# A gate in front of the third group's loads, a last copy and store in two halves, and a new order, in an RWKV attention and SmeLU feed-forward kernel

## The chip, the core and the metric

The kernel runs on one core of a Trainium2 chip. The metric is the device time of one execution in microseconds (us). The core has five engines that run their own instruction queues in order and wait for each other by semaphores: TensorE (PE, with its weight loads, PEld), VectorE (DVE), ScalarE (ACT), GpSimd (POOL) and SyncE (SP), which here only issues DMAs.

## What is computed

The reference takes r, k, v of shape (4, 8, 768, 48), a decay w and a bonus u per head and channel, and two weight matrices. It runs a linear attention with a decaying state over 768 positions, puts the heads of a position side by side (384 channels), and sends the 3072 rows through a feed-forward layer:

```python
for t in range(S):
    cur = einsum('bhd,bhe->bhde', u * k[t], v[t])
    y[t] = einsum('bhd,bhde->bhe', r[t], state + cur)
    state = w * state + einsum('bhd,bhe->bhde', k[t], v[t])
h = x @ w_in                      # x: (3072, 384), w_in: (384, 2048)
g = where(h >= 1, h, where(h <= -1, 0, (h + 1) ** 2 / 4))
out = g @ w_out                   # w_out: (2048, 384)
```

## The kernel before

The positions are cut into 6 chunks of 128 and the 4 batch rows into 2 pairs, which gives 12 groups. A group has two units (one batch row of one chunk: 128 positions, 8 heads). For a group the kernel makes scaled copies of r and k (Rs, Ks: r times a rising, k times a falling power of w), the bonus term (KU = k u, RKU = r KU, `us` sums it over channels, B multiplies it into v, giving V2), turns Rs and Ks so that channels lie on partitions (T, TR, TK on TensorE, or RT, KT by a DMA transpose from group 4 on), and multiplies them to A, the 128 x 128 matrix of each head. AT is A under a triangular mask in bf16. Y is AT times v, plus Rs times the state; `y` adds V2. Sp is the chunk's own contribution to the state, which Tm and decay fold in. Each y is turned to xT (X and xc, or by a DMA transpose, xcg).

The feed-forward layer goes in four pieces q of 512 hidden columns: m (12 matmuls of 256 columns, L464) into a pair of PSUM banks, then r and s (the clamped square on ScalarE, r sometimes on VectorE), then g on VectorE (L487), then M (per unit 4 matmuls of 384 columns, L499) into the output banks. A word such as M0.12 in the order is group 0, unit 1, piece 2. After the last M of a group, o or og copies the result out of PSUM and st or stg stores it through SP. For the last group (11) the two units are copied and stored apart.

w_in comes in three pieces (1, 1 and 2 of the four q, L243), w_out in two (2 and 2, L246), both through GpSimd's queue, which turns float32 into bf16 on the way. All loads of r, k and v (L252) go through SP in the order of the words LR, LK, LV. Groups 0 to 2 are loaded in half pieces (one unit), most of the others whole. Word Z issues filler matmuls on a tile of zeros (L526).

There is no scheduler. ORDER is a list of words, each one step, and the engines' queues follow the order of the words. A word may name the PSUM banks after a slash and the engine after "=" (V, A or G for VectorE, ScalarE, GpSimd). Buffers come from pools with a fixed number of slots (SLOTS), and a step that takes a slot again waits for the readers of what was in it. In this order the loads of group 2 (LR2.0, LR2.1) stand right behind the three words for w_in, followed on SP by LK2.0, LK2.1, LK3 and LR3.

Of the kernel before, what the change touches and what calls it, by code (L numbers as in the profile page):

```python
# [24 lines left out]
Zs/0 ln Z19 bw/1 LK0.0 bu/0 uS=V LK1.0 LR0.0 LK0.1 LR0.1 LV0.0 wq/2 WdnS Ks1.0=G LR1.0 LR1.1 Wdn/3 Ks0.0=V Ks0.1=V  # L25
TK0/0 Wup/1 Rs0.0=V TR0/3 LK1.1 cK0=A WupS KU0.1=G KU0.0=V RKU0.0=G cR0=A KU1.0=G LV0.1 Rs0.1=V Z2 TR1/1 A0/03 LV1.0
LV1.1 WI0 WI1 WI2 us0.0 cR1=A TK1/1 cK1=A AT0.1 Z4 A1/13 Rs1.0=V LR2.0 LR2.1 Rs1.1=V V0.1 AT1.0 V0.0 Z9 TR3/1 B0.0=G
AT1.1 RKU0.1=V wE AT0.0 wC=A us0.1 Z7 Y1/3 TR2/0 B0.1=G Y0/2 y0 y1 cR2=A RKU1.0=G Z8 X0/2 Z4 TK2/3 X1/0 Ks1.1=G xc0=A
Sp1/2 cK2=A xc1=A Z7 TK3/3 cK3=A Tm1 A2/20 m0.0/0 cR3=V us1.0 AT2.1 AT2.0 r0.0=A A3/31 AT3.1 KU1.1=G RKU1.1=G m0.1/1
V1.0 s0.0=A B1.0=G Sp2/2 AT3.0 us1.1 r0.1=A Tm2 Y2/3 y2 g0.0 V1.1 X2/0 LK2.0 Y3/1 B1.1=G s0.1=A LK2.1 Sp0/2 Sp3/3  # L30
xc2=V LK3 y3 WO0 m0.3/0 r0.3=A s0.3=A g0.1 X3/1 Tm0 xc3=V m0.2/1 LR3 LV2.0 Tm3 m1.1/2 g0.3 r1.1=V m1.0/3 m1.2/0 Ks2=G
r0.2=A s0.2=A g0.2 sbf2=A s1.1=A r1.0=A s1.0=A sbf3=A g1.1 m1.3/1 r1.2=V WO1 KU2=G LV2.1 M0.00/2 M0.10 M0.11 M0.01
g1.0 M1.00/3 M1.10 M1.11 M1.01 Rs2=G s1.2=A g1.2 T5/0 RKU2=G LK4 r1.3=A s1.3=A g1.3 T4/1 LV3 Ks3=G M0.02 M0.03 LR4 us2
c5=V A5/0 KU3=G Rs3=G c4=V A4/1 AT5 sbf1=A M1.02 M0.12 M0.13 AT4 T6/0 sbf0=A V2 Y4/1 Y5 B2=G og0=A T7/2 c6=A RKU3=G
c7=A yg2 LV5 M1.12 Sp4/0 Sp5 M1.03 X5/2 Tmg2 decayg2=G X4/1 M1.13 A6/0 xc4=A xc5=V m2.0/2 A7/1 us3 AT6 m2.1/0 og1=A
LK5 LR5 V3 Y6/3 B3=G sbfg2=A r2.0=A AT7 Y7 m2.2/1 s2.0=A Ks4=G yg3 xcg3 m2.3/3 g2.0 Rs4=G r2.1=A s2.1=A g2.1 LV4
r2.2=A s2.2=A KT4 M2.00/2 M2.10 M2.01 M2.11 r2.3=A KU4=G RT4 RKU4=G g2.2 s2.3=A LK6 m3.0/0 us4 M2.02 m3.1/1 LR6 M2.12
LV6 r3.0 s3.0=A Ks5=G g2.3 M2.03 Sp6/3 Sp7 M2.13 g3.0 m3.2/0 Rs5=G Tmg3 r3.1 s3.1=A RT5 og2=A g3.1 V4 AA4/23 AT9 Ks6=G
r3.2 s3.2=A KT5 m3.3/1 M3.00/3 M3.10 V5 B4=G AT8 Y8/2 Y9 r3.3 g3.2 s3.3=A LK8 M3.11 M3.12 M3.01 M3.02 yg4 AA5/20 g3.3
M3.13 M3.03 xcg4 m4.0/1 LR7 KU5=G RKU5=G AT10 LK7 decayg3=G sbfg3=A Rs6=G og3=A us5 LV7 B5=G KU6=G RKU6=G r4.0 Sp8/2  # L40
Sp9 AT11 Tmg4 m4.1/3 s4.0=A Y10/0 Y11 yg5 m4.2/2 r4.1 g4.0 xcg5 RT6 s4.1=A g4.1 m4.3/0 r4.2 us6 KT6 r4.3 LV8 s4.2=A
g4.2 M4.00/1 M4.10 M4.01 stg0 M4.11 s4.3=A g4.3 m5.1/3 Ks7=G V7 M4.12 LR8 decayg4=G Rs7=G AA6/02 M4.02 M4.03 M4.13
r5.1 AT12 m5.0/0 s5.1=A V6 sbfg4=A stg2 AT13 Y12/2 Y13 stg1 og4=V m5.2/1 g5.1 KU8=G B6=G yg6 m5.3/3 KT7 xcg6 Sp10/2
r5.0 s5.0=A KU7=G RKU7=G r5.2 s5.2=A Sp11 g5.0 M5.00/0 M5.10 M5.11 M5.01 RT7 Tmg5 LR9 g5.2 M5.02 Ks8=G LK9 us7 r5.3
s5.3=A V8 g5.3 decayg5=G sbfg5=A LK11 m6.1/2 r6.1 s6.1=A stg3 Rs8=G RT8 B7=G AA7/13 M5.03 Rs9=G M5.12 M5.13 AT15
m6.0/3 og5=A r6.0 AT14 g6.1 Y14/0 Y15 yg7 RKU8=G KU9=G xcg7 s6.0=A m6.3/1 m6.2/2 g6.0 Sp12/0 Sp13 r6.3 r6.2 s6.2=A us8
# [8 lines left out]
us11 AA11/12 B11=G r10.0 s10.0=A AT23 M9.12 M9.03 M9.13 AT22 m10.1/2 g10.0 sbfg9=A Y22/1 Y23 og9=A r10.1 stg9 s10.1=A
yg11 xcg11 m10.3/0 M10.00/3 g10.1 M10.10 r10.3 m10.2/1 s10.3=A g10.3 r10.2 M10.11 M10.01 s10.2=A m11.0/2 g10.2 r11.0
m11.1/0 M10.02 M10.03 r11.1 s11.0=A m11.2/1 g11.0 M10.12 M10.13 s11.1=A r11.2 g11.1 m11.3/2 og10=V s11.2=A M11.10/0
M11.11 g11.2 stg10 r11.3 s11.3=A M11.00/3 M11.01 M11.12 M11.02 g11.3 M11.13 M11.03 o11.1=V st11.1 o11.0=A st11.0
# [15 lines left out]
def kernel(  # L74
# [35 lines left out]
    def copy(e, out, in_):  # L110
        nc.scalar.copy(out, in_) if e == "A" else engines[e].tensor_copy(out, in_)  # L111
# [20 lines left out]
    idle = const.tile([P, 512], BF16, name="idle")  # L132
# [116 lines left out]
    def load(x, what, cls, g, j):  # L249
        j0, j1 = by_unit(g, j)  # L250
        t = make(cls, (what, g), [P, UNITS * H, D], F32)
        nc.sync.dma_start(out=t[:, j0 * H : j1 * H, :], in_=source(x, g, j0, j1))  # L252

# [237 lines left out]
    def do_M(e, b, g, jq):  # L491
        j, q = jq
        last = g == S // C * BP - 1
        key, k = (("op", g, j), 0) if last else (("op", g), j)
        if key not in tiles:
            tiles[key] = pair(b[0], F32, "op")
        wi, wo = part(q, OUT_PARTS)
        for f in range(FG):
            nc.tensor.matmul(  # L499
                tiles[key][:, k, :DO], tiles["g", g, q][:, f, j * P : (j + 1) * P], w_out_sb[wi][:, wo, f * DO : (f + 1) * DO],  # L500
                start=(q == 0 and f == 0), stop=(q == nQ - 1 and f == FG - 1),
            )
# [21 lines left out]
    def do_Z(e, b, n):  # L524
        for i in range(n):
            nc.tensor.matmul(tiles["z"][:, 0, :P], idle[:, :P], idle[:, :P], start=True, stop=True)  # L526

# [39 lines left out]
```

## Time and profile before

| | |
|---|---|
| median of 3 runs | 174.8 us (174.24 to 174.95) |
| the profiled execution's own time | 173.8 us |
| its span, first to last instruction | 172.0 us |
| TensorE busy | 163.7 us (95%) |
| VectorE, ScalarE, GpSimd busy | 130.6, 130.0, 117.1 us |
| DMA | 28.26 MB, 103591 packets, mean 164 GB/s |
| last matmul's end to the span's end | 3.5 us |

Times in the profile count from the start of the span. A row of the timeline gives start, length, engine, line, operation, output and inputs, shapes, and in brackets the idle time of the engine ahead of it with what ended that wait. "x3" says that a row stands for three neighbours. A row of DMA issues says when the issuing engine handed the transfer over; "DMA to landing" is the time from there until its data had arrived (least, median, most). The program's filler matmuls count as busy TensorE time.

### The profile page before, as it was taken

The page shows a single profiled execution, that of the slowest core. Times are in us where ns is not written, and L with a number is a line of the kernel's source. Part 1 is how long each engine was busy: PE and PEld are TensorE (multiplying, and loading weights), DVE is VectorE, ACT ScalarE, POOL GpSimd, SP SyncE. Part 2 cuts the span into 40 slices and gives each one's busy share as a digit, 9 for nine tenths or more (in the row PEclk, how much of TensorE's full clock was granted, in tenths as well). Part 3 has the DMA queues.
Part 4 walks back from the last instruction along what each step waited for, and adds up shares of the span by engine and source line. Part 5 has one row for each costly group of instructions (what it writes and reads, how often), then busy time and mean ns, then how long its engine had stood idle before and what let it go on. Part 6 is the DMA issues. An engine that isn't in the chain of part 4 may idle for free.

```text
span 172.0 us, 4014 instructions
## 1 busy us (share of the span) xinstructions
PE 163.7 (95%) x1658; PEld 130.9 (76%) x1658; DVE 130.6 (76%) x149; ACT 130.0 (76%) x150; POOL 117.1 (68%) x85
## 2 busy tenths in 40 slices
PE   7989968999999999989999999999999999999991
PEld 5768768956889778588787797696897787888850
DVE  4578798988687688859799779885889958873751
ACT  4356588991699899289979878689695896988941
POOL 3496755998589959999999998999577804300000
PEclk9999999999999999999999999999999999999999
DMA  5999999999995999999999998998999034130022
GB/s 106 198 187 191 199 203 197 221 195 203 174 190 88 213 188 175 188 204 150 200 312 197 185 215 174 219 173 168 308 195 219 4 60 138 43 98 0 8 91 91
DMA packets 103591, 28.26 MB, mean 164 GB/s; under 512 B 98834, under 2 KB 102676, under 8 KB 103572
## 3 DMA queue, kind: packets, MB, share of 16 engines
q1 hardware_dynamic: 101824, 24.85, 79.6%
q0 software_dynamic: 1744, 3.15, 10.0%
q8 instruction: 13, 0.21, 0.5%
q14 instruction: 6, 0.05, 0.1%
q10 hardware_dynamic: 4, 0.00, 0.0%
HBM read 20.45 MB, written 4.72 MB: 146 GB/s over the span
## 4 chain that ended last, share of the span: by engine, by line
PE 81%; DMA 5%; SPq 4%; ACT 3%; POOL 2%; DVE 2%; issue 1%; DVEq 0%; POOLq 0%
PE hp L464 36%; PE op L499 34%; SPq L252 4%; PE A L359 3%; DMA Vi<-in_v_dram 3%; DMA xT<-y 2%; PE Y L427 2%; PE Y L421 2%; PE Sp L394 2%; ACT pt L475 1%; ACT Vb L111 1%; POOL V L302 1%; PE T L319 1%; DVE g L487 1%; POOL RKU L271 1%
## 5 line engine op out<-in xcount | busy, mean ns | idle before, releaser
L464 PE MATMUL hp<-xT,w_in 128*128 128x256 bf16 x576 | 69.1, 273 | 0.9 <-DMA xT<-y 0.5
L499 PE MATMUL op<-w_out,g 128*128 128x384 bf16 x384 | 68.4, 326 | 0.0
L487 DVE SCALAR_TENSOR_TENSOR g<-sq,hp 128x1024 bf16<-128x1024 bf16 x48 | 57.9, 1215 | 13.2 <-ACT sq L484 13.2
L464 PEld LDWEIGHTS <-w_in 128*128 128x128 bf16 x576 | 61.9, 114 | 4.2 <-issue 1.2
L475 ACT ACTIVATE pt<-hp 128x1024 f32<-128x1024 f32 x46 | 46.9, 1020 | 14.0 <-PE hp L464 14.0
L499 PEld LDWEIGHTS <-g 128*128 128x128 bf16 x384 | 36.3, 98 | 21.3
L484 ACT ACTIVATE sq<-pt 128x1024 bf16<-128x1024 f32 x46 | 48.3, 1057 | 1.2
L368 DVE TENSOR_TENSOR AT<-A,umask 128x1024 bf16<-128x1024 f32 x20 | 23.7, 1219 | 5.2 <-PE A L359 5.2
L271 POOL TENSOR_TENSOR Ks<-Ki,Wdn 128x768 bf16<-128x768 f32 (+1 forms) x12 | 20.2, 1684 | 7.4 <-DMA Ki<-in_k_dram 3.7
L302 POOL TENSOR_TENSOR V<-Vb,diag 128x768 f32<-128x768 bf16 (+1 forms) x14 | 18.1, 1292 | 10.2 <-DVE diag L293 4.4
L271 POOL TENSOR_TENSOR RKU<-Ri,KU 128x768 f32<-128x768 f32 (+1 forms) x13 | 21.2, 1631 | 1.2 <-DVE KU L271 0.8
L405 POOL TENSOR_TENSOR state<-Tm,wCm 128x768 f32<-128x768 f32 x8 | 14.6, 1822 | 10.6 <-DVE Tm L402 10.6
L271 POOL TENSOR_TENSOR KU<-Ki,u_sb 128x768 f32<-128x768 f32 (+1 forms) x13 | 21.2, 1632 | 0.4 <-DMA Ki<-in_k_dram 0.3
L271 POOL TENSOR_TENSOR Rs<-Ri,Wup 128x768 bf16<-128x768 f32 x10 | 18.2, 1824 | 0.0
L439 DVE TENSOR_TENSOR y<-Y,V 128x768 bf16<-128x768 f32 x10 | 9.6, 956 | 5.9 <-PE Y L427 3.3
L111 ACT CAST Vb<-Vi 128x768 bf16<-128x768 f32 (+1 forms) x14 | 10.2, 734 | 4.8 <-DMA Vi<-in_v_dram 4.8
L293 DVE TENSOR_REDUCE diag<-RKU 128x16 f32<-128x768 f32 (+1 forms) x14 | 11.6, 830 | 1.5 <-POOL RKU L271 1.5
L111 ACT COPY o<-op 128x768 f32<-128x768 f32 (+1 forms) x9 | 6.9, 764 | 6.4 <-PE op L499 6.3
L111 ACT CAST state_bf<-state 128x768 bf16<-128x768 f32 (+1 forms) x12 | 8.5, 717 | 3.7 <-POOL state L405 3.7
L427 PE MATMUL Y<-Vb,AT 128*128 128x48 bf16 x192 | 10.2, 185 | 0.4 <-ACT Vb L111 0.4
L427 PEld LDWEIGHTS <-AT 128*128 128x128 bf16 x192 | 9.3, 97 | 0.7 <-issue 0.5
L402 DVE TENSOR_TENSOR Tm<-Sp,state 128x768 f32<-128x768 f32 x8 | 7.6, 956 | 2.7 <-PE Sp L394 2.7
(73 smaller groups left out, 121.2 us busy)
## 6 DMA issues: line engine op xcount, KB each, us to landing
out_dram<-o SPq DMA_DIRECT2D x11, 384.0 KB, 3.9
Ki<-in_k_dram SPq DMA_DIRECT2D x9, 384.0 KB, 6.0
Ri<-in_r_dram SPq DMA_DIRECT2D x9, 384.0 KB, 6.1
Vi<-in_v_dram SPq DMA_DIRECT2D x9, 384.0 KB, 5.0
w_out<-in_moe_w_out_dram POOLq DMA_DIRECT2D x2, 768.0 KB, 8.6
Ki<-in_k_dram SPq DMA_DIRECT2D x6, 192.0 KB, 3.9
Ri<-in_r_dram SPq DMA_DIRECT2D x6, 192.0 KB, 4.6
Vi<-in_v_dram SPq DMA_DIRECT2D x6, 192.0 KB, 5.4
```

The lines of the kernel that those rows point to most:

```text
L111: nc.scalar.copy(out, in_) if e == "A" else engines[e].tensor_copy(out, in_)
L271: engines[e].tensor_mul(part(out)[:, :, :, :D], part(a), rep(b, j1 - j0) if len(b.shape) == 3 and b.shape[1] == H else part(b))
L293: nc.vector.tensor_reduce(d[:, hs], tiles["RKU", g][:, hs, :], AX.X, ALU.add)
L302: engines[e].tensor_mul(t[:, hs, :], tiles["V", g][:, hs, :], tiles["diag", g][:, hs].unsqueeze(2).to_broadcast([P, n, D]))
L368: nc.vector.tensor_mul(t.rearrange("p i n t -> p (i n) t"), tiles["A", n].rearrange("p i (n t) -> p (i n) t", t=P), umask.unsqueeze(1).to_ ...
L405: engines[e].tensor_mul(states[g % BP], tiles["Tm", g], flat(wCm).unsqueeze(1).to_broadcast([P, UNITS, DM]))
L427: nc.tensor.matmul(Y[:, h * D : (h + 1) * D], AT[:, i, p, :], V[:, j * H + h, :], start=(c == 0), stop=True, skip_group_check=True,)
L464: nc.tensor.matmul(hp[:, f, :], w_in_sb[wi][:, i, wo * FG * P + f : (wo + 1) * FG * P : FG], tiles["xT", g][:, :, i, :], start=(i == 0), s ...
L475: nc.scalar.activation(t, tiles["hp", g, q], AF.Relu, bias=0.5, scale=0.5)
L484: nc.scalar.activation(t, p, AF.Square)
L487: nc.vector.scalar_tensor_tensor(out=make("g", ("g", g, q), [P, FG, TOK], BF16), in0=tiles["sq", g, q], scalar=1.0, in1=tiles["hp", g, q], ...
L499: nc.tensor.matmul(tiles[key][:, k, :DO], tiles["g", g, q][:, f, j * P : (j + 1) * P], w_out_sb[wi][:, wo, f * DO : (f + 1) * DO], start=( ...
```

## The change

Four things are edited.

The order is a new list. It holds the same steps for the same groups, apart from what is named here, and moves them within the engines' queues. Some steps change engine: RKU of group 2 and Ks and KU of group 3 go from GpSimd to VectorE, Rs of group 1's second unit from VectorE to GpSimd, the copy uS from VectorE to ScalarE. There are 65 filler matmuls instead of 60, with 10 instead of 19 at the very start.

A new word HR2 writes one element of the buffer that group 2's r will be loaded into, on VectorE. The load LR2.0 stands behind it in the list, so SP waits for it; all later loads stand behind LR2.0 on SP.

The last group's unit 1 is done in two column halves of 192: M puts them in two banks of its pair, the words MA and MB do the last piece half by half, and each half has its own copy (oA on ScalarE, oB on VectorE) and store (stA through ScalarE's queue, stB through SP). Unit 0 is finished before.

The tile of zeros shrinks from 512 to 128 columns. (HK and Zq are new words that the order does not use.)

```diff
-ORDER: ... LV1.0 LV1.1 WI0 WI1 WI2 us0.0 cR1=A TK1/1 cK1=A AT0.1 Z4 A1/13 Rs1.0=V LR2.0 LR2.1 Rs1.1=V ...
-       ... Y2/3 y2 g0.0 V1.1 X2/0 LK2.0 Y3/1 B1.1=G s0.1=A LK2.1 Sp0/2 Sp3/3 xc2=V LK3 y3 WO0 ...
-       ... M11.11 g11.2 stg10 r11.3 s11.3=A M11.00/3 M11.01 M11.12 M11.02 g11.3 M11.13 M11.03 o11.1=V st11.1 o11.0=A st11.0
+ORDER: ... WI0 WI1 A0/01 AT0.1 V0.0 wE wC=A LV1.1 Z3 TK1/2 cK1=A Rs1.0=V WI2 ...
+       ... Y2/0 r0.0=A m0.1/0 Tm2 AT3.0 us1.1 y2 X2/3 s0.0=A r0.1=A HR2=V LR2.0 Sp0/2 LK2.0 LK2.1 V1.1 Sp3/0 g0.0 ...
+       ... g11.3 M11.03 MA11.13 MB11.13 o11.0=V st11.0 oA11.1=A stA11.1=A oB11.1=V stB11.1
-    idle = const.tile([P, 512], BF16, name="idle")
+    idle = const.tile([P, P], BF16, name="idle")
+    def gate(e, what, cls, g):
+        engines[e].memset(make(cls, (what, g), [P, UNITS * H, D], F32)[:1, :1, :1], 0.0)
+    def do_HR(e, b, g):
+        gate(e, "R", "Ri", g)
-    def do_M(e, b, g, jq):
+    def do_M(e, b, g, jq, halves=(0, 1)):
...
+        for i, o0, o1 in [(i, i * DO // 2, (i + 1) * DO // 2) for i in halves] if last and j else [(j, 0, DO)]:
+            for f in range(FG):
+                nc.tensor.matmul(
+                    tiles[key][:, i, : o1 - o0], tiles["g", g, q][:, f, j * P : (j + 1) * P], w_out_sb[wi][:, wo, f * DO + o0 : f * DO + o1],
+                    start=(q == 0 and f == 0), stop=(q == nQ - 1 and f == FG - 1),
+                )
+    def half_out(e, g, j, i):
+        cols = slice(i * DO // 2, (i + 1) * DO // 2)
+        copy(e, make("o", ("o", g, j), [P, UNITS, DO], F32)[:, 0, cols], tiles["op", g, j][:, i, : DO // 2])
+    def half_st(e, g, j, i):
+        cols = slice(i * DO // 2, (i + 1) * DO // 2)
+        (nc.scalar if e == "A" else nc.sync).dma_start(out=rows_out(g, j, j + 1)[:, :, cols], in_=tiles["o", g, j][:, 0:1, cols])
```

VectorE's queue around the memset, before: AT of group 1's last unit, the sums and y of its first, then g of group 0. (AT's input A_405 is group 1's second unit, `pt` is r on VectorE, `state` is Tm.)

```order
L373 TENSOR_TENSOR AT<-A_405,umask 128x512
L293 TENSOR_REDUCE diag<-RKU 128x8
L398 TENSOR_TENSOR state<-Sp,wCm 128x384
L435 TENSOR_TENSOR y<-Y,V_436 128x384
L487 SCALAR_TENSOR_TENSOR g<-sq,hp 128x1024
L111 COPY xT<-X 128x384
L435 TENSOR_TENSOR y<-Y,V_436 128x384
L487 SCALAR_TENSOR_TENSOR g<-sq,hp 128x1024
```

And in the new order, from the same y on:

```order
L446 TENSOR_TENSOR y<-Y,V_410 128x384
L257 MEMSET Ri 1x1
L498 SCALAR_TENSOR_TENSOR g<-sq,hp 128x1024
L384 TENSOR_TENSOR AT<-A_418,umask 128x512
L112 COPY xT<-X 128x384
L446 TENSOR_TENSOR y<-Y,V_410 128x384
L498 SCALAR_TENSOR_TENSOR g<-sq,hp 128x1024
L409 TENSOR_TENSOR state<-Sp,wCm 128x384 x2
```

The memset stands between y and the first g, and one AT of group 1 has moved behind that g.

GpSimd's queue around the two issues of w_out, before:

```order
L302 TENSOR_TENSOR V_436<-Vb,diag 128x384 x2
L246 DMA w_out_119<-in_moe_w_out_dram 128x2x1536
L271 TENSOR_TENSOR Ks<-Ki,Wdn 128x16x48
L246 DMA w_out_120<-in_moe_w_out_dram 128x2x1536
L271 TENSOR_TENSOR KU<-Ki,u_sb 128x768
```

And in the new order (V_410 is V2 of group 1, both Ki are group 2's k):

```order
L313 TENSOR_TENSOR V_410<-Vb,diag 128x384 x2
L247 DMA w_out_119<-in_moe_w_out_dram 128x2x1536
L282 TENSOR_TENSOR KU<-Ki,u_sb 128x768
L247 DMA w_out_120<-in_moe_w_out_dram 128x2x1536
L282 TENSOR_TENSOR Ks<-Ki,Wdn 128x16x48
```

KU and Ks of group 2 have changed places; each is the first to need group 2's k, and the second issue of w_out stands behind it.

VectorE's queue a little later, before, where `pt` is the r of group 1's third piece:

```order
L472 TENSOR_SCALAR pt<-hp 128x1024
L487 SCALAR_TENSOR_TENSOR g<-sq,hp 128x1024 x3
L293 TENSOR_REDUCE diag<-RKU 128x16
L111 COPY TT<-T 128x1024 x2
L368 TENSOR_TENSOR AT<-A,umask 128x1024 x2
```

And in the new order, with the products of groups 2 and 3 that were GpSimd's:

```order
L483 TENSOR_SCALAR pt<-hp 128x1024
L498 SCALAR_TENSOR_TENSOR g<-sq,hp 128x1024
L282 TENSOR_TENSOR RKU<-Ri,KU 128x768
L498 SCALAR_TENSOR_TENSOR g<-sq,hp 128x1024 x2
L282 TENSOR_TENSOR Ks<-Ki,Wdn 128x16x48
L282 TENSOR_TENSOR KU<-Ki,u_sb 128x768
L379 TENSOR_TENSOR AT<-A,umask 128x1024
L304 TENSOR_REDUCE diag<-RKU 128x16
L379 TENSOR_TENSOR AT<-A,umask 128x1024
```

RKU, Ks and KU are new on VectorE, and two copies of T have left it for ScalarE.

More of the change, by code (lines that the diff above doesn't have):

```diff
@@ L24 @@
 ORDER = """
[L25 to L34, printed above, removed]
@@ L55 @@
[L55 to L58, printed above, removed]
+Zs/0 LK1.0 LR0.0 LK0.0 ln Z10 bw/0 Wup/1 WdnS LK1.1 LR0.1 bu/3 Wdn/1 LK0.1 Ks1.0=V wq/2 uS=A KU0.0=G RKU0.0=G KU1.1=G
@@ L526, in do_Z, with do_Zq @@
             nc.tensor.matmul(tiles["z"][:, 0, :P], idle[:, :P], idle[:, :P], start=True, stop=True)
+    def do_Zq(e, b, n):
+        for i in range(n):
+            nc.tensor.matmul(tiles["z"][:, 0, :D], idle[:, :P], idle[:, :D], start=True, stop=True)
     steps = {name[3:]: f for name, f in locals().items() if name.startswith("do_")}
```

78 lines of the change are left out of this document (51 added, 27 removed).

## The prediction, made before the run

> **What bounds the kernel now.** I read the windows first. They cut the span at the points where TensorE's work changes; the columns are stretch, length, then busy time (and instructions) of PE, PEld, DVE, ACT and POOL, the clock, the DMA share and GB/s.
>
> ```profile
> 10.69:27.09 16.40, 13.64 (x180) 11.79 (x180) 13.97 (x25) 10.29 (x19) 10.42 (x13) 1.00 1.19 196
> 27.09:60.00 32.91, 32.91 (x336) 26.44 (x336) 26.39 (x28) 26.41 (x32) 28.54 (x17) 1.00 1.06 184
> 60.00:100.00 40.00, 39.53 (x415) 31.15 (x414) 33.25 (x32) 33.18 (x36) 37.37 (x23) 1.00 1.12 200
> 100.00:160.00 60.00, 60.00 (x623) 49.00 (x622) 45.45 (x42) 49.20 (x53) 35.38 (x21) 1.00 0.71 141
> 168.50:172.00 3.50, 0.01 (x1) 0.00 (x0) 0.00 (x0) 0.48 (x1) 0.00 (x0) 1.00 0.32 112
> ```
>
> Second, the chain that ended last, at the pieces used below.
>
> ```profile
> 25.91 1.14 DVE g L487
> ...
> 27.09 6.73 PE hp L464 x60
> 33.82 5.20 PE op L499 x32
> 39.02 0.89 PE T L319 x16
> ...
> 44.27 0.04 PE Y L421
> ...
> 46.11 0.34 PE Sp L394 x8
> ...
> 168.54 0.48 ACT o L111
> ```
>
> From 27.09 to about 168.5 us TensorE misses only 40.00 − 39.53 = 0.47 us. The matmuls themselves are the same in both kernels, so the span of 172.0 us has three places that can move: the 27.09 us before the dense stretch, waits that come up inside it, and the 3.5 us behind the last matmul. The dense stretch is released by VectorE (the g that ends at 27.05), and VectorE is busy 13.97 of the last 16.40 us before it. The start is a VectorE chain more than a TensorE one, since part of TensorE's 13.64 us there are the filler matmuls on zeros.
>
> **The start: when does the dense stretch begin?** In the new order TensorE does five of the eight groups of transposes of the first two groups of rows, and more fillers, before the first A. These rows price that.
>
> ```profile
> 7.76 0.61 PE L319 MATMUL TK<-ident,Ks 128*128 128x128 bf16 x4
> 10.04 0.61 PE L359 MATMUL A<-TT 48*128 48x128 bf16 x8
> 12.58 1.14 PE L526 MATMUL z<-idle 128*128 128x128 bf16 x9
> 15.52 0.61 PE L526 MATMUL z<-idle 128*128 128x128 bf16 x8
> 7.09 0.99 POOL L271 TENSOR_TENSOR KU<-Ki,u_sb 128x384 f32<-128x384 f32 x1 [0.35 <-DMA Ki<-in_k_dram]
> 10.75 2.47 POOL L243 DMA_DIRECT2D w_in<-in_moe_w_in_dram  x3
> 10.69 0.69 DVE L373 TENSOR_TENSOR AT<-A,umask 128x512 bf16<-128x512 f32 x1 [0.25 <-PE A L359]
> 11.30 1.01 DVE L271 TENSOR_TENSOR Rs<-Ri,Wup 128x384 bf16<-128x384 f32 x2
> 1.73 0.08 DVE L139 CAST i_col<-i_int 128x1 f32<-128x1 int32 x1
> 13.89 0.55 DVE L271 TENSOR_TENSOR RKU<-Ri,KU 128x384 f32<-128x384 f32 x1
> ```
>
> Five matmuls more cost 1.14 − 0.61 = 0.53, so 0.106 us each at this point, and the tail of a group is 0.61 − 4 x 0.106 = 0.19. From 7.76 on the new order runs 20 transposes and 19 fillers ahead of the first A: 39 x 0.106 = 4.1, so A starts at 11.9 and is through at 12.5, against 10.65 before. GpSimd must have made the second half of group 1's Ks by then: four products of 0.99 from 7.09 on end at 11.0, so it has, and w_in is issued at 11.0 instead of 10.75.
>
> VectorE then runs from that A to the same g. Its work in the window before was 13.97. One Rs (half of 1.01) and one RKU (0.55) leave the stretch, and the memset of one element adds no more than the cast of one column, 0.08. That is 13.0 of work. The waits before were 16.40 − 13.97 = 2.4. Placing the new rows one after the other I find four: the second unit's A (0.3), Tm behind the first m (0.5), y behind the last Y (0.2), small ones (0.3). So the g ends at 12.55 + 13.0 + 1.3 = 26.85 and the dense stretch begins at 26.9, 0.2 earlier. With all of before's waits it is 28.0 (0.9 later). Were TensorE quicker in the transposes, the first A could still not be through before about 11.7, since it stands behind the transposes of that Ks, which ends at 11.0: then 26.1 (1.0 earlier with equal waits).
>
> **The held loads.** Before, the loads of group 2 are issued beside w_in.
>
> ```profile
> 11.88 3.79 SPq L252 DMA_DIRECT2D Ri<-in_r_dram  x2
> DMA to landing us min/median/max: 5.5/8.4/11.9
> 25.26 0.76 POOL L246 DMA_DIRECT2D w_out<-in_moe_w_out_dram  x1
> 29.59 0.76 POOL L246 DMA_DIRECT2D w_out<-in_moe_w_out_dram  x1
> DMA to landing us min/median/max: 8.3/8.6/8.9
> 27.80 1.84 POOL L271 TENSOR_TENSOR Ks<-Ki,Wdn 128x768 bf16<-128x768 f32 x1 [1.78 <-DMA Ki<-in_k_dram]
> ```
>
> The first landing row is w_in's three pieces, issued 0.8 apart (2.47/3) from 10.75 on: they land at 16.3, 20.0 and 24.3. The last piece has as many elements as each half of w_out (3 x 1024 against 2 x 1536) and takes 4.3 us behind the one before it. The halves of w_out land at 33.6 and 38.5, 4.9 apart, with hardly a load landing in between (below). So the loads beside it do not visibly slow w_in, and what releases the dense stretch is a g, not w_in: I put the gain from holding them back at nothing. The Trainium skill (DMA: Bandwidth & Descriptors, Queues, rings and completion order) says that each DMA engine alternates between queues packet by packet; by that w_in should have been slowed by the loads' share, and these landings do not show it.
>
> What the hold costs: VectorE reaches the memset behind y of unit 2, in my placing at 22.7. SP waits there, and every later load with it. Three loads bring group 2's K (R half, K, K). Before, the first three loads into an empty queue went like this; the landing row is for the second and third.
>
> ```profile
> 0.74 1.08 SPq L252 DMA_DIRECT2D Ki<-in_k_dram  x2
> 1.87 0.76 SPq L252 DMA_DIRECT2D Ri<-in_r_dram  x1
> DMA to landing us min/median/max: 3.6/3.8/4.0
> 8.61 3.23 SPq L252 DMA_DIRECT2D Vi<-in_v_dram  x3
> 25.14 2.83 SPq L252 DMA_DIRECT2D Ri<-in_r_dram  x1
> DMA to landing us min/median/max: 14.0/14.0/14.0
> 41.03 0.83 ACT L111 CAST Vb<-Vi 128x768 bf16<-128x768 f32 x1 [2.51 <-DMA Vi<-in_v_dram]
> 41.58 2.35 DVE L368 TENSOR_TENSOR AT<-A,umask 128x1024 bf16<-128x1024 f32 x2 [0.57 <-PE A L359]
> 38.88 0.94 DVE L293 TENSOR_REDUCE diag<-RKU 128x16 f32<-128x768 f32 x1
> ```
>
> The third landed 1.87 + 4.0 − 0.74 = 5.1 after the first was issued, so K lands at 22.8 + 5.1 = 27.9, about as before (27.8). KU now stands ahead of the second w_out issue on GpSimd, where Ks stood: 27.9 + 1.84 = 29.7 against 29.59, landing 8.3 to 8.9 later, 38.0 to 38.6. TensorE wants that half at its turn of M0.12: 26.9 + 6.73 + 7 x 0.65 (5.20/8) + 0.45 = 38.6. A tie.
>
> The loads behind are later. Before, group 3's R was issued at 25.14, was caught by w_out and landed 14.0 later, at 39.1. In the new order group 3's K takes its place, so 39.1 for that. A half load takes 1.08 on the queue (3.23/3), so R follows two of them later at 41.3, and V is as much later than its 41.0 of before, 43.2; its cast ends at 44.0. K is the tighter one: RKU, Ks and KU of groups 2 and 3 have moved from GpSimd to VectorE, about 1.0 each (two of 0.55, less overlap), and Ks waits for K on VectorE with both AT behind it. 39.1 + Ks 1.0 + KU 1.0 + AT 1.2 + diag 0.9 + AT 1.2 = 44.4. Y of group 2 has its turn at 44.27 − 0.2 + 0.34 (Sp now ahead of it) = 44.4, and Sp, which needs V, at 44.1. Two more ties; for all three together I take 0.4; bounds 0 (K lands in the gap between the halves of w_out) and 2.2 (K at 41.3, where I have R).
>
> **The dense stretch otherwise.** The wait of 0.47 is that of m4.0 on its xT; the new order has the same six M and two A between that y and m4.0, so it stays. The Ms of unit 1 in the last group are now 192 wide, twice as many, with twice the weight loads. If a matmul's time goes by width this costs nothing, and at one weight load each it costs:
>
> ```profile
> L499 PEld LDWEIGHTS <-g 128*128 128x128 bf16 x384 | 36.3, 98 | 21.3
> ```
>
> 32 x 0.098 − 16 x 0.1625 = 0.5. The transposes (0.89/16 = 0.056 with a load each) are the nearer row, so I take 0.05.
>
> **The end.** Before, the last copy takes 0.48 and its store lands 1.9 later:
>
> ```profile
> 168.48 0.91 SPq L515 DMA_DIRECT2D out_dram<-o  x2
> DMA to landing us min/median/max: 1.9/1.9/1.9
> ```
>
> Now the last piece is half as wide: the copy saves between 0 and 0.24, I take 0.17. The other unit's copy on VectorE is covered by the two half Ms (0.65). The half store saves between 0 and 0.95; most of a store this small is not bytes, so I take 0.15. With the 0.05 above the end is 0.3 earlier.
>
> **The sum.** −0.2 + 0.4 − 0.3 = −0.1. The profiled execution took 173.8 (span 172.0 and 1.8 around it) and becomes 173.7; the median of the runs is 174.8, 1.0 higher, so I forecast 174.7. About 0.5%, 0.87 us, is what a measurement of this kernel can tell from no change.
>
> **Rivals.** *The start gains in full.* Fillers go from 0.127 each (1.14/9) to 0.076 (0.61/8) between 12.6 and 15.5, while the windows print a clock of 1.00 throughout. The new order packs 13 fillers in a row just ahead of the first A. If the doubling comes before them, A is through at 11.7 and the start is 1.0 earlier; VectorE's waits hold some of it, so 0.9. With K in time (0) and 0.3 at the end: 173.6. For it: fewer holes on TensorE from 7.76 on. Against: before was busy too and doubled late. The Trainium skill (TensorE: Matmul & The Clock Gate, Part 1) tells of a free-running window of about 3.4 us that must be busy; by that the point is one of phase, and the trace shows only that it lay near 15.
>
> *Group 2's K misses the gap ahead of w_out (slower).* The first w_out issue follows group 1's last V2 on GpSimd, in my placing at 24.8, 2 us behind the gate. If the gate opens some tenths later than that, the end of K is caught as group 3's R was. KU, the second w_out half and M0.12 stand behind it in a row, and from K at 28.5 (38.6 − 8.3 − 1.84) on each us of K is a us of TensorE. Caught throughout it lands with w_out at 24.8 + 8.3 = 33.1, 4.7 us; caught for half of that, 2.4, in place of the 0.4: 176.7. For it: 14.0 against 4.0 us to landing. Against: all three loads would be in flight 2 us ahead. The rule of the Trainium skill (DMA: Bandwidth & Descriptors, Rules for kernel authors) to issue a DMA early and wait for it late speaks on this side; no run shows it yet.
>
> *The hold does not help and nothing else does:* that is my forecast's own view of the hold, and without the start's 0.2 it gives 174.9.
>
> **How the numbers follow.** Forecast (with the third case) 0.46, its own range 173.9 to 175.6; full start 0.33; K caught 0.18; the remaining 0.03 to a wait that I do not see. Faster by over 0.5% (under 173.9) takes the full start and little of the forecast: 0.36. Slower (over 175.7) takes K caught and the forecast's worse end (start 0.9 later, K of group 3 late): 0.24. Same: 0.40. The range leaves out the case with every bound good (1.0 at the start, 0.24 and 0.95 at the end: 172.6) and the upper half of K caught: 173.0 to 176.4.
>
> **What would show it.** Right: the g before the dense stretch ends near 26.9; w_in's last piece still takes 4 us or more behind the one before; K of group 2 at about 27.9; TensorE misses 0.2 to 1 us between 38 and 46; under 3.3 us behind the last matmul. Wrong: a dense stretch that begins before 26.2 or after 27.6; w_in landing over 1 us earlier and m starting on it; TensorE waiting over 1 us for w_out, or new waits beyond 50 us, for which I have no term.

## The result, and the profile after

The changed kernel takes 175.42 us (median of 19 runs, 174.68 to 177.0), the kernel before in the same session 174.47 (19 runs, 173.98 to 175.25). The ratio is 1.0056, with a 95% interval of 1.0037 to 1.0076: slower by about 1.0 us, a little over the half per cent that can be told from no change. The profiled execution took 175.65 with a span of 173.9; the one of before took 173.8 with 172.0. So the two traces differ by 1.9 us where the medians differ by 1.0: one trace of each overstates the loss, and I read places from the traces and sizes from the medians and ratios. The medians and ranges given here are of all executions, the ratios leave out those that fell into a slower state of the chip, so the two need not agree (nogate's 177.05 is 1.0135 times the median beside it, its ratio 1.0095).

First the windows of the changed kernel, the same stretches as before the change and then the end.

```profile
10.69:27.09 16.40, 14.24 (x196) 11.98 (x194) 14.89 (x27) 11.36 (x20) 10.82 (x13) 1.00 1.09 177
27.09:60.00 32.91, 32.15 (x330) 25.66 (x328) 27.52 (x29) 26.10 (x30) 23.39 (x15) 1.00 1.06 188
60.00:100.00 40.00, 39.36 (x411) 30.59 (x410) 31.82 (x30) 32.63 (x36) 34.76 (x21) 1.00 1.06 198
100.00:160.00 60.00, 59.23 (x615) 48.16 (x614) 48.05 (x45) 48.12 (x51) 37.85 (x22) 1.00 0.73 146
170.39:173.90 3.51, 0.00 (x0) 0.00 (x0) 0.36 (x1) 0.32 (x1) 0.00 (x0) 0.94 0.34 112
```

Before, TensorE missed nothing from 27.09 to 60 and from 100 to 160, and 0.47 between; now it misses 0.76, 0.64 and 0.77. The end behind the last matmul is 3.5 us as it was. Of what TensorE waits for over the whole span, these two rows lie inside the dense stretch (us, times, longest):

```profile
PE hp L475 <- DMA xT<-y: 1.4, 3, 0.8
PE op L512 <- DMA w_out<-in_moe_w_out_dram: 0.8, 1, 0.8
```

The start and the first new wait, at single instructions in order of time (start, length, what; in brackets the idle time ahead and what ended it):

```profile
24.53 1.48 PE L475 MATMUL hp<-xT,w_in 128*128 128x256 bf16 x12
26.54 1.69 PE L475 MATMUL hp<-xT,w_in 128*128 128x256 bf16 x14 [0.36 <-DVE g L498]
28.48 1.83 POOL L282 TENSOR_TENSOR KU<-Ki,u_sb 128x768 f32<-128x768 f32 x1 [3.03 <-DMA Ki<-in_k_dram]
30.26 0.76 POOL L247 DMA_DIRECT2D w_out<-in_moe_w_out_dram  x1
39.02 1.46 PE L512 MATMUL op<-w_out,g 128*128 128x384 bf16 x8 [0.76 <-DMA w_out<-in_moe_w_out_dram]
```

The dense stretch starts at 26.54 instead of 27.09. Group 2's K is there at 28.48 (before 27.80), the second issue of w_out goes out at 30.26 (before 29.59), and the matmuls that need it stand still for 0.76 us. The view of the tile w_in gives its three pieces from issue to landing:

```profile
DMA to landing us min/median/max: 6.6/8.0/10.7
```

Issued 0.8 apart from 11.0 on, they land at 17.6, 19.8 and 23.4, the last 3.6 behind the one before it, where it was 4.3.

The waits on xT are three now. The longest is that of m7.1, and SP's row in time ahead of it shows why:

```profile
97.54 1.31 SPq L253 DMA_DIRECT2D Ri<-in_r_dram  x1
98.90 4.65 SPq L253 DMA_DIRECT2D Ki<-in_k_dram  x2
103.68 2.71 SPq L318 DMA_TRANSPOSE RT<-Rs  x1
106.49 1.23 SPq L467 DMA_TRANSPOSE xT<-y  x1
```

Beside it, its y on VectorE and the matmuls that wait:

```profile
102.43 0.96 DVE L450 TENSOR_TENSOR y<-Y,V 128x768 bf16<-128x768 f32 x1 [0.68 <-POOL V L313]
109.33 0.84 PE L475 MATMUL hp<-xT,w_in 128*128 128x256 bf16 x6 [0.77 <-DMA xT<-y]
```

Its y is there at 103.39, but SP is in two loads of K until 103.55 and then takes the transpose of RT, 2.71 us; that of xT goes out at 106.49, 3.1 after its y. In the kernel before, the same three stood in the same order on SP, but these loads went out earlier, with a store behind them, and SP was through with RT when y (ended at 102.52) was there:

```profile
94.09 3.67 SPq L252 DMA_DIRECT2D Ki<-in_k_dram  x2
...
100.38 2.17 SPq L307 DMA_TRANSPOSE RT<-Rs  x1
102.66 1.22 SPq L456 DMA_TRANSPOSE xT<-y  x1
```

At the wait of 0.24 near 83 the new order has put an RT of 2.47 ahead of xT, which stood first. The wait of 0.40 near 74 is the 0.47 of before.

### The profile page after: what moved, and what is told of

Its sections match the earlier page's. It is cut to its first block, busy times and chain, and to the rows that moved or that the text cites. A ratio compares the mean times of both kernels' runs of the same rounds, so it can differ in the third digit from the quotient of the medians.

```text
span 173.9 us, 4069 instructions
## 1 busy us (share of the span) xinstructions
PE 163.9 (94%) x1679; PEld 131.7 (76%) x1679; DVE 134.3 (77%) x153; ACT 130.9 (75%) x151; POOL 111.9 (64%) x82
## 4 chain that ended last, share of the span: by engine, by line
PE 66%; DMA 16%; POOL 5%; ACT 4%; DVE 4%; issue 2%; SPq 2%; DVEq 0%; POOLq 0%
PE hp L475 28%; PE op L512 28%; DMA xT<-y 5%; DMA w_out<-in_moe_w_out_dram 5%; DMA Ri<-in_r_dram 3%; PE A L370 3%; DMA Ki<-in_k_dram 2%; PE Y L438 2%; PE Y L432 2%; PE Sp L405 2%; SPq L253 2%; POOL w_in L244 1%; ACT pt L486 1%; ACT sq L495 1%; POOL KU L282 1%
## 5 line engine op out<-in xcount | busy, mean ns | idle before, releaser
L512 PE MATMUL op<-w_out,g 128*128 128x384 bf16 (+1 forms) x400 | 68.3, 320 | 0.8 <-DMA w_out<-in_moe_w_out_dram 0.8
L512 PEld LDWEIGHTS <-g 128*128 128x128 bf16 x400 | 37.4, 98 | 21.6 <-issue 0.9
L282 POOL TENSOR_TENSOR KU<-Ki,u_sb 128x768 f32<-128x768 f32 (+1 forms) x12 | 19.5, 1625 | 7.8 <-ACT u_sb L112 4.7
L282 POOL TENSOR_TENSOR Rs<-Ri,Wup 128x768 bf16<-128x768 f32 (+1 forms) x11 | 19.3, 1755 | 5.9 <-DMA Ri<-in_r_dram 5.0
L282 POOL TENSOR_TENSOR RKU<-Ri,KU 128x768 f32<-128x768 f32 (+1 forms) x12 | 19.4, 1617 | 0.1
L282 POOL TENSOR_TENSOR Ks<-Ki,Wdn 128x768 bf16<-128x768 f32 (+1 forms) x10 | 17.5, 1746 | 0.3 <-PE Sp L405 0.3
L112 ACT COPY o<-op 128x768 f32<-128x768 f32 (+1 forms) x8 | 5.9, 742 | 6.9 <-PE op L512 6.8
```

The costliest lines, as they stand in the source:

```text
L282: engines[e].tensor_mul(part(out)[:, :, :, :D], part(a), rep(b, j1 - j0) if len(b.shape) == 3 and b.shape[1] == H else part(b))
L512: nc.tensor.matmul(tiles[key][:, i, : o1 - o0], tiles["g", g, q][:, f, j * P : (j + 1) * P], w_out_sb[wi][:, wo, f * DO + o0 : f * DO + o1 ...
```

## The experiments

Each time stands beside runs of the kernel before on the same chip, and all ratios are to it; the changed kernel's own is 1.0056. My theory was that two places share the loss, the memset's (K of group 2 and w_out behind it) and the new row of transposes on SP; the first rival, that the held loads are late everywhere and the waits on xT are their echo. What each would give is in the expectations; the letters A and B mean something else in each of them. In these diffs of the order, words that are left out stay where they were.

**The hold taken out of the new order, and put alone into the old one.**

nogate:

```diff
-... s0.0=A r0.1=A HR2=V LR2.0 Sp0/2 ...
+... s0.0=A r0.1=A LR2.0 Sp0/2 ...
```

> The changed kernel without the memset that holds back group 2's loads. Theory A (three places of their own: w_out's second half issued late behind group 2's KU, transposes of xT queued on SP, a tail that gains nothing): K of group 2 is in before 28, the wait of 0.8 us on w_out goes, the waits on xT (0.4, 0.2, 0.8 us) stay, and w_in's last piece takes 4.3 us again instead of 3.6, so that the third m may wait 0.2: about 0.6 faster than the changed kernel, 1.002 of before. Theory B (the late loads push everything behind them on SP, so the waits on xT are their echo): the waits on xT go too, 1.7 faster than the changed kernel, 0.995 of before.

Measured 177.05 (174.93 to 180.15), ratio 1.0095 (1.0055 to 1.0136), where theory A had 1.002. The memset is not the loss: without it the kernel is no faster. K of group 2 comes at 26.79 and the wait on w_out goes, but:

```profile
25.04 1.50 PE L475 MATMUL hp<-xT,w_in 128*128 128x256 bf16 x12 [0.63 <-DMA w_in<-in_moe_w_in_dram]
73.77 1.47 PE L475 MATMUL hp<-xT,w_in 128*128 128x256 bf16 x12 [0.54 <-DMA xT<-y]
83.27 1.47 PE L475 MATMUL hp<-xT,w_in 128*128 128x256 bf16 x12 [0.41 <-DMA xT<-y]
109.23 1.50 PE L475 MATMUL hp<-xT,w_in 128*128 128x256 bf16 x12 [0.77 <-DMA xT<-y]
```

m0.3 now waits 0.63 for w_in, whose last piece takes 12.3 from its issue to landing instead of 10.7. And all three waits on xT are there without the hold, so they are not a late echo of the held loads. Six of the twelve executions have a mean granted clock of 0.99 and took 176.96 to 180.15; the other six, with a clock of 1.00 as in all 19 of the changed kernel, took 174.93 to 177.14, five of them under 176. The profiled execution is of the second kind, so its trace does not show where the clock fell.

before_gate, where group 2's loads wait for a memset behind y2 and all else is the old order:

```diff
-... Rs1.0=V LR2.0 LR2.1 Rs1.1=V ...
+... Rs1.0=V Rs1.1=V ...
-... Y2/3 y2 g0.0 V1.1 X2/0 LK2.0 ... LK2.1 Sp0/2 ...
+... Y2/3 y2 HR2=V LR2.0 g0.0 V1.1 X2/0 LK2.0 ... LK2.1 LR2.1 Sp0/2 ...
```

> The kernel before with the gate alone: the one-element memset behind y of group 1's first unit, and group 2's loads behind it in the changed kernel's order. Theory A: K of group 2 lands 0.7 later and w_out's second half with it, but in this order TensorE asks for that half 1.4 us after it landed, so nothing waits: 0.999 to 1.002 of before. w_in's last piece lands 3.6 after the one ahead of it instead of 4.3. Theory B: everything on SP behind the loads is 2 us late, and TensorE waits on xT or V: 1.005 or more.

Measured 178.23 (175.79 to 178.68), ratio 1.0151 (1.01 to 1.0203), slower than theory A had it. VectorE reaches this memset later, the first load goes out at 23.70, and K of group 2 no longer comes ahead of w_out:

```profile
32.63 1.83 POOL L278 TENSOR_TENSOR Ks<-Ki,Wdn 128x768 bf16<-128x768 f32 x1 [6.60 <-DMA Ki<-in_k_dram]
34.41 0.76 POOL L247 DMA_DIRECT2D w_out<-in_moe_w_out_dram  x1
42.15 2.54 PE L506 MATMUL op<-w_out,g 128*128 128x384 bf16 x8 [2.23 <-DMA w_out<-in_moe_w_out_dram]
```

The window from that wait on, whose third last column is the granted clock:

```profile
42.00:46.00 4.00, 3.85 (x27) 1.95 (x27) 1.46 (x3) 0.83 (x1) 4.00 (x4) 0.57 1.26 199
```

K comes at 32.63 (28.48 in the changed kernel, gate 1.1 us earlier), TensorE waits 2.23, and behind the wait the granted clock is 0.57 on average for 4 us: eight matmuls take 2.54 instead of 1.46. This is the prediction's slow rival, with a part that it did not have. Four of the six executions have a mean granted clock of 0.99 (178.15 to 178.68); the other two took 175.79 and 176.56, so that about 2 us of the loss go with the clock.

**w_out's second half ahead of KU**, in the new order, so that it does not stand behind K:

```diff
-... WO0 KU2=G s0.2=A g0.3 m1.2/3 r1.1=V WO1 ...
+... WO0 WO1 KU2=G s0.2=A g0.3 m1.2/3 r1.1=V ...
```

> The changed kernel with w_out's second issue moved ahead of group 2's KU on GpSimd. Theory A: the wait of 0.8 us on w_out goes; the loads of group 3 get less room between the two halves, so that up to 0.5 may come back at group 2's Y: 0.3 to 0.8 faster than the changed kernel, 1.001 to 1.004 of before. Theory B (late loads are the cause): the loads are later still, so no gain or 0.3 slower than the changed kernel, 1.006 to 1.008.

Measured 176.75, ratio 1.0111 (1.0083 to 1.014): slower than the changed kernel, and than either theory had it. The wait on the second half goes, but with both halves in flight the loads behind starve: the second half of group 2's R lands 12.8 behind its issue instead of 9.3, GpSimd's product of it starts at 37.47 instead of 33.75, and TensorE waits for that:

```profile
40.10 0.40 PE L330 MATMUL T<-ident,Rs 128*128 128x128 bf16 x4 [1.67 <-POOL Rs L282]
```

So an issue held back behind K is not only a cost: the gap that it leaves is what the loads use.

**The memset three VectorE operations earlier** (ahead of an AT, the sums and y; the expectations say two), in the new order:

```diff
-... Tm2 AT3.0 us1.1 y2 X2/3 s0.0=A r0.1=A HR2=V LR2.0 Sp0/2 LK2.0 LK2.1 ...
+... Tm2 HR2=V LR2.0 LK2.0 LK2.1 AT3.0 us1.1 y2 X2/3 s0.0=A r0.1=A Sp0/2 ...
```

> The changed kernel, with the memset and the three loads behind it two VectorE operations further ahead, so that the first load is issued at about 21.1 us instead of 22.6. Theory A (the hold is a trade between w_in's last piece and K of group 2 in the gap ahead of w_out): K of group 2 is there at 27.0 to 27.3 instead of 28.5, the second half of w_out is issued at about 29.0 instead of 30.3, the wait of 0.76 at M0.12 goes, w_in's last piece lands 0.2 to 0.6 later, with it m0.3 and the dense stretch up to 0.3, and the time falls by 0.4 to 0.8 us to 174.6 to 175.0. Rival B (the wait at M0.12 is w_out's own pace, not the issue behind K): the second half lands at 38.8 to 39.2 as now, and the time stays or grows with the start, 175.4 to 176.0.

Measured 174.93, ratio 1.002 (0.9991 to 1.0049), as theory A had it. K at 26.50, no wait for w_out, and w_in's last piece no later than in the changed kernel (10.6). It is about 0.6 below the changed kernel; the intervals just overlap.

```profile
26.50 1.82 POOL L282 TENSOR_TENSOR KU<-Ki,u_sb 128x768 f32<-128x768 f32 x1 [1.62 <-DMA Ki<-in_k_dram]
28.28 0.76 POOL L247 DMA_DIRECT2D w_out<-in_moe_w_out_dram  x1
```

**xT ahead of RT on SP**, in the new order, in two places (the words RT6 and RT8 moved behind xcg5 and xcg7):

> The changed kernel, with SP issuing the transpose of xT ahead of that of RT in two places (units 5 and 7 of xT, ahead of RT of groups 6 and 8). Theory A (half of the loss is SP's row of transposes, each held 2 to 3 us on the queue): the waits of hp on xT near 83 and 109 us (0.24 and 0.77) go, the one near 74 (0.40) stays, and the time falls by 0.8 to 1.0 us to about 174.5. Rival B (the y that the transposes read is late in the new order, and SP's row only shows it): the waits come back within 0.2 us of what they were, elsewhere or on RT, and the time stays at 175.2 to 175.6.

Measured 174.98, ratio 1.0025 (0.9997 to 1.0052): about 0.5 below the changed kernel, where 0.8 to 1.0 was expected. The waits near 83 and 109 are gone. In their stead KT is waited for once: it stands behind both on SP in either order, and TensorE now comes to it sooner:

```profile
74.91 1.47 PE L475 MATMUL hp<-xT,w_in 128*128 128x256 bf16 x12 [0.52 <-DMA xT<-y]
111.23 0.62 PE L370 MATMUL A<-RT,KT 48*128 48x128 bf16 x16 [0.57 <-DMA KT<-Ks]
```

**Both mends together**, xt_gate:

> The changed kernel with the two mends that did not touch the end: xT ahead of RT on SP in two places, and the memset two operations earlier. Theory A (they add up, 0.5 and 0.6 under the changed kernel's 1.0056): 174.0 to 174.4, ratio 0.997 to 1.000. Rival B (one takes over what the other gives): ratio 1.002 or more.

Measured 174.47, ratio 0.9989 (0.9956 to 1.0022): they add up, to the time of before and not below it.

**The end.** before_halves is the old order with the end in halves, as the change has them:

```diff
-... M11.01 M11.12 M11.02 g11.3 M11.13 M11.03 o11.1=V st11.1 o11.0=A st11.0
+... M11.01 M11.12 M11.02 g11.3 M11.03 MA11.13 MB11.13 o11.0=V st11.0 oA11.1=A stA11.1=A oB11.1=V stB11.1
```

> The kernel before with the last group's unit 1 in two halves and nothing else. Theory A: the copies of the two halves follow each other because they share a tile, so the end lies 3.5 us behind the last matmul as before: 0.999 to 1.001. Rival: the halves do save 0.3 and the changed kernel lost it elsewhere: 0.998.

Measured 174.37, ratio 0.9991 (0.9966 to 1.0016): no gain that can be told, though 0.3 us would lie within the interval; in its trace the span ends 3.48 behind the last matmul. The end of the changed kernel shows why the halves do not overlap:

```profile
164.99 5.40 PE L512 MATMUL op<-w_out,g 128*128 128x192 bf16 x48
170.43 0.32 ACT L112 COPY o<-op 128x192 f32<-128x192 f32 x1 [3.13 <-PE op L512]
170.78 0.38 ACTq L539 DMA_DIRECT2D out_dram<-o  x1
170.78 0.36 DVE L112 COPY o<-op 128x192 f32<-128x192 f32 x1 [0.45 <-ACT o L112]
171.16 0.34 SPq L539 DMA_DIRECT2D out_dram<-o  x1
```

ScalarE's copy of the first half waits for the matmuls of the second (the last matmul ends at 170.39), and VectorE's copy waits for ScalarE's: both halves share a PSUM tile and an output tile, and these waits go by tile. So I gave each half tiles of its own:

```diff
-        key = ("op", g, j) if last else ("op", g)
+            key = ("op", g, j, i) if last and j else ("op", g, j) if last else ("op", g)
-make("o", ("o", g, j), ...)  tiles["op", g, j]
+make("o", ("o", g, j, i), ...)  tiles["op", g, j, i]
```

In own_tiles the second half's PSUM pair is the one that group 10's result has left:

> The changed kernel, with the two halves of the last unit in PSUM tiles and output tiles of their own. Theory A (the halves gained nothing because the program's waits go by tile: the first half's copy waits for the second half's matmuls, and VectorE's copy for ScalarE's): the first half's copy starts before the last matmul is through, VectorE's copy starts within 0.1 of the last matmul, and the span ends 3.1 to 3.2 us behind the last matmul instead of 3.5, so 0.35 us less than the changed kernel, 175.1. Rival B (the end is the time of a small store whatever stands before it): VectorE's copy starts earlier but the span still ends 3.4 to 3.5 behind the last matmul, and the time stays within 0.1 of 175.4.

In own_banks it is that of m11.3 (M11.0 goes ahead of the second half's first two pieces); before_own_banks does the same in the old order, with the pair of m11.2:

> The halves in tiles of their own once more, with the second half's PSUM tile in the pair that m11.3 has left (in own_tiles it was the pair of group 10's result, and TensorE waited 1.5 us for its copy), so that nothing new is waited for. Theory A (the halves gained nothing because they shared tiles): the last copy starts within 0.1 of the last matmul, the span ends 3.1 to 3.3 behind it, 0.2 to 0.4 below the changed kernel: 175.0 to 175.2, ratio 1.003 to 1.005. Rival B (the end is a small store's own time, as own_tiles already hints with 3.4 behind the last matmul): 3.4 to 3.5 again, ratio 1.005 to 1.006.

> The kernel before, with the end in halves that have tiles of their own. Theory A: 0.2 to 0.4 us faster than before, ratio 0.998 to 0.999, more than the halves in shared tiles gave there (0.9991, not told from 1). Rival B: nothing again, 0.9985 to 1.0015 with the span ending 3.4 to 3.6 behind the last matmul.

Measured 177.01, ratio 1.0154 (1.0107 to 1.02); 176.56, ratio 1.0118 (1.0084 to 1.0152); 175.35, ratio 1.0057 (1.0036 to 1.0078). All three are slower, for a reason that neither theory had: there is no free PSUM pair there. TensorE waits 1.5 us for the copy of group 10's result in the first, and in own_banks for the last g, which still reads m11.3:

```profile
168.09 3.44 PE L512 MATMUL op<-w_out,g 128*128 128x192 bf16 x32 [1.06 <-DVE g L498]
170.91 1.02 DVE L112 COPY o<-op 128x384 f32<-128x384 f32 x2 [2.87 <-PE op L512]
171.24 0.32 ACT L112 COPY o<-op 128x192 f32<-128x192 f32 x1 [4.45 <-PE op L512]
171.95 0.36 SPq L539 DMA_DIRECT2D out_dram<-o  x1
```

(The first half's copy on ScalarE runs beside the second half's matmuls here, as meant; VectorE's, the last 0.36 of the group of 1.02, follows the last matmul at once.) The question of the end is answered all the same: the last matmul ends at 171.53 and the span at 175.0, 3.47 behind it, and 3.46 in before_own_banks. That is rival B's number, but not quite its reason. The view of the half stores of the changed kernel, and then of own_banks:

```profile
DMA to landing us min/median/max: 1.7/1.7/1.8
DMA to landing us min/median/max: 2.0/2.1/2.1
```

A whole store took 1.9. With tiles of their own the last store goes out 0.42 behind the last matmul, sooner than in the changed kernel (0.77), but it lands that much later. Why the half stores take longer there is not shown; they follow unit 0's store by 0.09 and 0.46, where it was 0.43 and 0.81.

all_three and three_fixed joined these ends to both mends, and show only that: 1.0082 (1.0045 to 1.012) with the wait of 1.5, and 1.01 (1.0068 to 1.0133) with that of 1.06, above 0.9989 for the mends alone.

> The three edits together on the changed kernel: halves in tiles of their own, xT ahead of RT on SP in two places, the memset two operations earlier. Theory A: they lie in three places of the span and add up, 0.35 + 0.9 + 0.6 = 1.85 below the changed kernel, 173.6, 0.5% below the kernel before. Rival B (what TensorE does not wait for in one place it waits for in the next): less than half of the sum, 174.6 or more.

> On the changed kernel: the halves as in own_banks, xT ahead of RT on SP in two places, the memset two operations earlier. Theory A (three places, which add up): xt_first and gate_early lay 0.5 and 0.6 us under the changed kernel, with 0.2 for the end 1.3 in all: 174.1 to 174.3, ratio 0.996 to 0.998. Rival B (a wait that goes comes back behind): ratio 1.000 or more.

**The new start with the old order behind it.** Up to m0.2 and the three words behind it the list is the changed kernel's, from m1.1 on that of before (with w_out's first issue and two loads just ahead of m1.1, and with pairs 0 and 1 exchanged throughout, since the start leaves them so); the last copy and store are whole. What the expectations call the tenth input step is this place. splice has the memset as early as gate_early:

> The changed kernel's order up to the tenth MoE input step (with the memset two operations earlier, as in gate_early), and from there on the order of the kernel before; the last copy and store whole. Theory A (the new start is worth 0.55 or more, the hold costs nothing when it opens early enough, and the rest of the loss is the new order behind 45 us): TensorE's dense stretch starts at 26.0 to 26.5, at most one wait on xT (0.5), no wait for w_out, and the time is 0.5 to 1.0 below before: 173.6 to 174.1, ratio 0.994 to 0.997. Rival B (what the start gains comes back wherever the loads of groups 2 and 3 are late, whatever the order behind): waits for V or R of group 3 at 43 to 46 us of 0.5 or more, and a ratio of 0.998 to 1.003.

Measured 174.18 (173.01 to 175.12), ratio 0.9973 (0.9953 to 0.9993). Then the memset where the change has it, and no memset:

> As splice, but the memset stands where the change has it: new start unmodified, from the tenth MoE input step on the old order, whole last copy and store. Theory A (the memset's place costs about 0.6, the order behind 45 us about 0.9): w_out is waited for at M0.1x by 0.5 to 1.0, at most one wait on xT, time 174.5 to 174.9, ratio 1.000 to 1.002. Rival B (the place of the memset makes no difference; it is all the order behind): ratio 0.996 to 0.998, as splice.

> As splice, without the memset, so that group 2's loads go out as soon as their buffers are free. Theory A (the hold is worth the 0.6 that m0.3 otherwise waits for w_in, if it opens early): m0.3 waits for w_in again by 0.4 to 0.8, the dense stretch starts near 26.5, ratio 0.999 to 1.002. Rival B (the hold is worth nothing, the start's gain is the order's): ratio 0.996 to 0.998, as splice.

splice_late took 174.0, ratio 0.9953 (0.9924 to 0.9983): faster than both kernels. splice_nogate took 174.73, ratio 0.9986 (0.9961 to 1.0012). The start of splice_late and w_out's issue in time:

```profile
26.13 2.12 PE L475 MATMUL hp<-xT,w_in 128*128 128x256 bf16 x18 [0.20 <-DVE g L498]
27.73 1.82 POOL L282 TENSOR_TENSOR Ks<-Ki,Wdn 128x768 bf16<-128x768 f32 x1 [2.67 <-DMA Ki<-in_k_dram]
29.52 0.76 POOL L247 DMA_DIRECT2D w_out<-in_moe_w_out_dram  x1
```

TensorE's waits behind the start:

```profile
PE T L330 <- POOL Rs L282: 0.8, 1, 0.8
PE hp L475 <- DMA xT<-y: 0.4, 1, 0.4
```

The window of the later stretch:

```profile
100.00:160.00 60.00, 60.00 (x622) 48.99 (x621) 45.59 (x42) 49.21 (x52) 35.55 (x21) 1.00 0.72 142
```

There is no wait for w_out, though it is issued as late as 29.52, and from 100 to 160 TensorE misses nothing. Theory A had the memset's place cost 0.6 here too; it doesn't, since in the old order TensorE comes to w_out's second half later. Before, that was at 39.75; in the new order the turn was due at 38.26 (39.02 less the wait), because one M and one of two transposing steps (T4) had moved behind it.

Without the memset, m0.3 waits again, and in this execution the clock falls behind that wait:

```profile
24.72 2.53 PE L475 MATMUL hp<-xT,w_in 128*128 128x256 bf16 x12 [0.65 <-DMA w_in<-in_moe_w_in_dram]
```

The window around it:

```profile
24.00:28.00 4.00, 3.35 (x21) 2.45 (x19) 2.98 (x5) 1.04 (x2) 2.04 (x3) 0.63 1.06 192
```

The dozen takes 2.53 instead of 1.48. Of the twelve executions five have a mean granted clock of 0.99 (174.67 to 175.60), one took 240.16 at 0.67, and the other six took 173.99 to 174.78.

Both pairs of runs (1.0095 against 1.0056, 0.9986 against 0.9953) point to some half per cent that the hold is worth once the start is the new one, but the intervals overlap in both, so it is not settled. Nor does the hold always keep m from waiting for w_in. In xt_first's trace, with the memset, the last piece took 12.3 as well, and TensorE waited for w_in twice, the first time before the first held load went out (22.02):

```profile
21.24 1.50 PE L475 MATMUL hp<-xT,w_in 128*128 128x256 bf16 x12 [0.76 <-DMA w_in<-in_moe_w_in_dram]
25.07 1.50 PE L475 MATMUL hp<-xT,w_in 128*128 128x256 bf16 x12 [0.28 <-DMA w_in<-in_moe_w_in_dram]
```

## Why the prediction was wrong

It said 174.7 and no change; it is 175.42 and slower, inside the range. By its own steps:

- **The start**: the sign was right, the size too small. A was through at 12.7, as forecast (12.5). From there to the end of the g, at 26.48, VectorE had 12.90 of work, as forecast (13.0), and waited 0.9 instead of 1.3: of the four waits that I had placed, the trace lists two, Tm's (0.35) and y's (0.26). So the g came 0.55 earlier in the trace instead of 0.2. The rival "The start gains in full" did not come in this trace, but for the most part it did in others of the same instructions. The 13 fillers and the A, in the changed kernel and then in splice_late:

```profile
10.10 1.59 PE L566 MATMUL z<-idle 128*128 128x128 bf16 x13
12.05 0.61 PE L370 MATMUL A<-TT 48*128 48x128 bf16 x8
10.05 1.19 PE L566 MATMUL z<-idle 128*128 128x128 bf16 x13
11.74 0.40 PE L370 MATMUL A<-TT 48*128 48x128 bf16 x8
```

The matmuls double in speed behind the A in the first and among the fillers in the second. Of the thirteen traces with the new start, eight have the A through at 12.1 to 12.2 and five at 12.5 to 12.7; where no w_in was waited for, the dense stretch began at 25.96 to 26.31 in the former and 26.32 to 26.70 in the latter. The instructions up to there are the same in all thirteen, so it changes between executions; how often each came in those without a trace is not known. So no single trace sizes the start, and some of the difference between two kernels with this start, up to about 0.4 us, may be this. splice_late, which has this start and the old order behind, is 0.8 us faster than before by its ratio.
- **The held loads**: the step "the loads beside it do not visibly slow w_in" failed. I compared w_in's last piece with w_out's halves, which had loads beside them too (group 3's R, 25.14 to 39.1). Without the memset that piece takes 11.9 to 12.4 to land (five traces, old and new start), with it 10.6 to 12.3 (twelve traces, the middle at 11.4), and without it m0.3, which now comes earlier, waits 0.6 for it. Whether "I put the gain from holding them back at nothing" failed as well, in time, is not settled (above). The rule of the Trainium skill that I had set aside there (DMA: Bandwidth & Descriptors, Queues, rings and completion order), that each DMA engine takes turns between the queues packet by packet, fits this tendency; the two ranges overlap, so the runs do not show more than that.
- **K, the second half of w_out and its turn**: the chain was right and the "tie" was not. The first held load went out at 22.59, as placed (22.8), but the three loads took 5.9 instead of the 5.1 that I had read off the empty queue, so K came at 28.48 instead of 27.9, the issue at 30.26 instead of 29.7, the landing 8.7 later at 39.0, and the turn was due at 38.26 instead of 38.6: each a little to the wrong side, 0.76 in place of a share of the 0.4. The other two ties held: the trace lists no wait for R or at Y.
- **The dense stretch otherwise**: this step failed too. "The wait of 0.47 … stays" was true (0.40), but I looked at that wait alone and did not go down SP's queue, where in two more places xT now comes late behind an RT. Two more waits, 1.0 us in the trace; about 0.5 us comes back when xT goes first. The prediction had named this as what would make it wrong: new waits beyond 50 us "for which I have no term".
- **The halves' matmuls** cost what I took: 48 end in 5.40, where 32 took 5.36.
- **The end**: the step "0.3 earlier" failed, 3.5 as before. Of its two parts the store came as forecast, 0.1 to 0.2 sooner (1.7 to 1.8 against 1.9; 0.15 was taken). The copy did not: "the copy saves between 0 and 0.24" took it that the last copy starts with the last matmul's end, but VectorE's half waited for ScalarE's, which had waited for the last matmul, so the last store went out 0.77 behind that matmul instead of 0.5. The two cancel. The other unit's copy was covered, as forecast (169.77 to 170.33).

Sum of the ratios, in us: the start −0.8, the rest of the new order and the end +1.8 (1.0056 against 0.9953). Of this 1.8 the memset's place with the early turn took about 0.6 and SP's queue about 0.5 (gate_early, xt_first). Each alone is within the intervals; together (0.9989, at most 1.0022) they are clear of the changed kernel (1.0056, at least 1.0037). What is left between the mended new order and splice is 0.3 to 0.6, within the intervals; TensorE's busy time from its dense start to its end is 0.7 longer in the changed kernel's trace than in that of before (141.68 against 140.94), but 141.24 in xt_gate's and 141.25 in splice_late's, so that this is not the order's alone; what it is stays open.

## What to carry to other kernels

When a list of orders is searched anew, walk every queue of it and not only the waits of the old trace: a transfer that stands ahead of another on a queue costs its own time there, here 2.5 to 2.7 us for a transpose. Whether holding loads back pays depends on who comes next: price the held transfer's landing against the turn of whoever stands behind it in the new order (in this order K at 28.48 cost 0.76 and K at 26.50 nothing). Before splitting a last copy, ask what the halves share and what they would need: in shared tiles the copies followed each other, with tiles of their own TensorE waited 0.9 to 1.5 us for a free PSUM pair, and the end stayed at 3.4 to 3.5 us either way.

## What the runs showed of the hardware

A wait at or inside the dense stretch can cost more than its length. In the 4 us around a wait of 0.65 the granted clock was 0.63 on average, and the twelve matmuls behind the wait took 1.05 longer than elsewhere; in the 4 us behind a wait of 2.23 it was 0.57. But waits of 0.76 in the changed kernel and 0.63 in nogate's profiled execution left it at 1.00. What decides this is not shown here. At the start the matmuls doubled in speed sooner in some executions than in others of the same instructions, which put the first A 0.3 to 0.5 us apart. And loads that went out 1.1 us later at the gate (23.70 and 22.59), beside a large transfer issued at 25.27 and 24.69, had K in place 4.2 us later (32.63 and 28.48).
